# A fused scan and bilinear feed-forward kernel: pair 4's loads issued ahead of pair 0's stores, B and C of pairs 2 and 3 turned in two banks, pair 2's output copied in two halves, weights loaded in groups of three, no probe loads

## The chip, the cores and the metric

The kernel runs on one core of a Trainium2 chip. A core has four compute engines (TensorE, VectorE, ScalarE and GpSimd, in the profile PE, DVE, ACT and POOL) and SyncE (SP), which here only issues transfers. PEld is TensorE's loading of the stationary operand, which overlaps its matmuls. Each engine runs its own instructions in the order in which they were recorded, and waits on semaphores for the others. The metric is device time in microseconds, the median over runs of the whole kernel. This kernel's runs lie between 132.43 and 134.8 us.

## The reference

The first half is a gated linear recurrence (a Mamba-2 state space scan) over 4 batches of 8 heads, 768 positions, 32 channels per head and 16 states; the second is a bilinear feed-forward layer on the 3072 rows that come out.

```python
# per batch and head; log_a = log(clip(a)); chunks of positions
cum = cumsum(log_a)                       # within the chunk
M   = (C @ B.T) * exp(cum_i - cum_j) * (i >= j)
y   = M @ x + (C @ state) * exp(cum)
state = exp(sum(log_a)) * state + B.T @ (x * exp(cum_last - cum_j))
# then, with y of all heads side by side: X is 3072 x 256
out = ((X @ w_a) * (X @ w_b)) @ w_out     # w_a, w_b: 256 x 1536; w_out: 1536 x 256
```

## The kernel before

**Tiling.** The positions are cut in 6 blocks of 128. A *pair* is one block of two batches: pair p is block p // 2 of batches 2(p % 2) and 2(p % 2) + 1, so there are 12 pairs, 0 to 11, and pair p needs the state that pair p - 2 left. The decays are turned into factors (`fB`, `fC`), with which B and C are scaled; the rest is matmuls.

**What is done for one pair.** In this order, by function:

- `load(p)`: six transfers on SP's queue, two each of B (`bn`), C (`cn`) and x (`xn`), 64 KB, 64 KB and 128 KB. They go to a pool with three buffers of each.
- `scale(p)`: three GpSimd instructions, in this order: C times its factor (`cm`), B times its factor (`bm`), x to 16 bits (`x16`).
- `transposes(p)`: four TensorE transposes, B's two (`bm`) and then C's two (`cm`), into PSUM; then copies to SBUF: `BT` by two ScalarE instructions, one for each parity of the head, and `CT` by one. In the loop all three are on ScalarE. For pairs 2 and 3 `CT` is copied first, by VectorE (`ct_first`). B and C lie in the same PSUM bank, the first of the tile `SC0`.
- `scores(p)`: 32 small matmuls into the four banks of `SC0` and `SC1` (`SC[0]` to `SC[3]`; two banks belong to one tile).
- `mask(product(p, m))`: four instructions of 128x512, causal mask times scores, on VectorE. For pairs 0 to 2 one of the four goes by ScalarE (`tmp`) and GpSimd.
- `pv(p)`: scores times x, plus C times the old state (`Sbd`), into the two banks of `SC1`, and the new state's sum (`ds_mm`); then one ScalarE instruction of 128x512 copies the result to `X2T`.
- `state(p)`: two small VectorE instructions (`U32`) and two on GpSimd (`Sbd`, and `gU` for the pair after the next).
- `unit(p, k2)`, k2 from 0 to 5: four matmuls of 128x256 with `Wa` and four with `Wb` for two of the 12 tiles of hidden columns, a ScalarE copy of the first result (`asb`), and the VectorE product `hk`, which is `times`.
- `out_mm` and `out_store`: 12 matmuls of `hk` with `Wo` for each of the two batches of the pair, a ScalarE copy (`osb`) and a store on SP's queue.

**Order.** The order on each engine is written out by hand. From pair 3 on a loop interleaves the scores and masks of pair p with units of pair p - 1 and the output of pair p - 2; ahead of it, pairs 0 to 2 have their own straight-line order (lines 505 to 625), which the change touches. SP's queue there issues, in this order: pair 2's x, `load(3)`, the two stores of pair 0, `load(4)`, and then in the loop's first pass `load(5)`.

**Waits.** The layer that records the instructions adds the semaphores. For PSUM it works by tile: of two engines that use one tile the later waits for the earlier, also where both only read.

**Weights.** `Wa`, `Wb` and `Wo` come by GpSimd's queue in halves, and are turned from 32 to 16 bits on the way. The 12 tiles of 128 hidden columns are interleaved: partition c of tile k is a column of the weights so chosen that the rows of `w_out` that a partition takes lie side by side in memory. For `Wo` that is six rows (6 KB) for a partition and half; for `Wa` and `Wb` it means that the 128 weights of a partition which a matmul takes as its stationary operand lie six elements (12 bytes) apart.

**Probes.** Line 577 issues seven transfers of 64 bytes a row on SP's queue, ahead of pair 2's x. They go to a tile that nothing reads; the first waits for pair 1's x.

Of the kernel before, what the change touches and what calls it, by code (L numbers as in the profile page):

```python
# [9 lines left out]
f32 = mybir.dt.float32  # L10
f16 = mybir.dt.float16
u32 = mybir.dt.uint32
AF = mybir.ActivationFunctionType
ALU = mybir.AluOpType
PSUM = bass.MemoryType.PSUM
AFTER = mybir.DependencyInfo(mybir.DependencyClass.Sync, mybir.DependencyReason.DATA)

XS = 1024.0
YS = 16.0
# [3 lines left out]
def kernel(  # L23
# [13 lines left out]
    nc = tc.nc  # L37
# [27 lines left out]
    const = ctx.enter_context(tc.tile_pool(name="const", bufs=1))  # L65
# [16 lines left out]
    Wo = big.tile([128, NK, d_model], f16, name="Wo")  # L82
    X2T = big.tile([128, NP, 2, 2, Q], f16, name="X2T")
# [21 lines left out]
    SC1 = ps4.tile([128, 2, 512], f32, name="SC1")  # L105
    SC = [SC0[:, 0], SC0[:, 1], SC1[:, 0], SC1[:, 1]]
# [7 lines left out]
    def tiles(p):  # L114
        Bn = inp.tile([128, H, 2, N], f32, name="bn", tag="bn")
        Cn = inp.tile([128, H, 2, N], f32, name="cn", tag="cn")
        Xn = inp.tile([128, H, 2, D], f32, name="xn", tag="xn")
        pair_in[p] = (Bn, Cn, Xn)

    def load1(eng, p, which, bt, i0=0, n=64):  # L120
        blk, bp = divmod(p, NBP)
        src = (B, C, x)[which][2 * bp + bt, :, blk * Q + 2 * i0 : blk * Q + 2 * i0 + 2 * n, :]
        return eng.dma_start(
            pair_in[p][which][64 * bt + i0 : 64 * bt + i0 + n].rearrange("i h r n -> i h (r n)"),
            src.rearrange("h (i r) n -> i h (r n)", r=2),
        )

    def load(p, eng=None):
        tiles(p)
        return [load1(eng or nc.sync, p, w, bt) for w in range(3) for bt in range(2)]  # L130

    def load_w(half):
        c = slice(half * KC, (half + 1) * KC)
        return [
            nc.gpsimd.dma_start(W[half], src.rearrange("(f p) e -> p f e", p=128)[:, :, c])
            for W, src in ((Wa, moe_w_a), (Wb, moe_w_b))
        ]

    def load_wo(half):
        nc.gpsimd.dma_start(  # L140
            Wo[:, 6 * half : 6 * half + 6].rearrange("p kk e -> p (kk e)"),
            moe_w_out.rearrange("(g p kk) e -> p g (kk e)", p=128, kk=6)[:, half],
        )

    nc.sync.dma_start(a_sb, a.rearrange("b h (k q) -> (b h) k q", q=Q))
    for p_ in range(3):
# [16 lines left out]
        out=sel,  # L163
        in_=sel,
# [9 lines left out]
        out=ident, in_=ident, compare_op=ALU.is_equal, fill=0.0, base=0, pattern=[[-1, 128]], channel_multiplier=1  # L174
    )
    nc.gpsimd.memset(causal, 1.0)
    for bt in range(2):
        v = causal[64 * bt : 64 * bt + 64]
        nc.gpsimd.affine_select(  # L179
            out=v, in_=v, compare_op=ALU.is_ge, fill=0.0, base=0, pattern=[[-1, 2], [1, Q]], channel_multiplier=-2  # L180
# [1 line left out]
    load1(nc.gpsimd, 1, 0, 1)  # L182
    load1(nc.gpsimd, 1, 1, 0)
    load_w(0)
    x1 = [load1(nc.gpsimd, 1, 2, bt) for bt in range(2)]

    def warmup(n, bank, cols=512):
        for _ in range(n):
# [66 lines left out]
        scale_bc(p, 0, nc.gpsimd)  # L255
        scale_x(p, nc.gpsimd)

    def transposes(p, ps=None, between=None, ct_first=False):
        s = st[p]
        TB, TC = (TT[:, 0:256], TT[:, 256:512]) if ps is None else [t_.bitcast(f16)[:, 0:256] for t_ in ps]  # L260
        for T_, src in ((TB, s["bm"]), (TC, s["cm"])):
            for r in range(2):
                nc.tensor.transpose(  # L263
                    T_[:, r * 128 : (r + 1) * 128], src[:, r].rearrange("p h n -> p (h n)"), ident
                )
            if between:
                between()
                between = None
        BT = mid.tile([128, 2, 2, 2, 64], f16, name="bt", tag="bt")
        CT = mid.tile([128, 2, Q], f16, name="ct", tag="ct")  # L270

        def ct(copy):
            copy(CT.rearrange("p t (i r) -> p r (t i)", r=2), TC.rearrange("p (r c) -> p r c", r=2))

        if ct_first:
            ct(nc.vector.tensor_copy)
        for e in range(2):
            o_ = BT[:, e].rearrange("p r t i -> p (r t i)")
            nc.scalar.activation(out=o_, in_=TB, func=AF.Copy, scale=par[:, e : e + 1])  # L279
        if not ct_first:  # L280
            ct(nc.scalar.copy if ps is None else nc.vector.tensor_copy)
        s["BT"], s["CT"] = BT, CT

    def scores(p):
# [18 lines left out]
    def product(p, m):  # L303

        return (
            st[p]["T1"][:, 2 * m : 2 * m + 2].rearrange("p e r q -> p e (r q)"),
            SC[m].rearrange("p (e c) -> p e c", e=2),
        )
# [8 lines left out]
    def mask(out_in, by_pool=False):  # L317
        o_, i_ = out_in
        c_ = causal.rearrange("p r q -> p (r q)").unsqueeze(1).broadcast_to((128, 2, 2 * Q))
        if by_pool:  # L320
            tmp = mid.tile([128, 2, 2 * Q], f32, name="tmp", tag="tmp")
            nc.scalar.copy(tmp, i_)  # L322
            nc.gpsimd.tensor_tensor(out=o_, in0=tmp, in1=c_, op=ALU.mult)  # L323
        else:
            nc.vector.tensor_tensor(out=o_, in0=i_, in1=c_, op=ALU.mult)  # L325
# [32 lines left out]
                        tile_position=(64 * bt, 32 * m),  # L358
                    )

    def pv(p, then=None):
        blk, bp = divmod(p, NBP)
        s = st[p]
        PY = [SC1[:, bt, 0:256] for bt in range(2)]
        if blk > 0:
            for bt in range(2):
                for u in range(2):
                    nc.tensor.matmul(  # L368
                        PY[bt][:, u * Q : (u + 1) * Q],
                        s["Sbd"][:, bt, u * 128 : u * 128 + 128],  # L370
                        s["CT"][:, bt],
                        start=(u == 0),
                        stop=False,
                        skip_group_check=True,
                    )
        for u in range(2):
            pv_u(p, u, PY, blk == 0)
        if blk < NBLK - 1:
            ds_mm(p, 256)
        if then:  # L380
            then()
        nc.scalar.activation(  # L382
            out=X2T[:, p].rearrange("p u t q -> p t u q"),
            in_=SC1[:, :, 0:256].rearrange("p t (u q) -> p t u q", u=2),
            func=AF.Copy,
            scale=YS / XS,
        )

    def evac0(u, bt, eng, py):
        o_, i_ = X2T[:, 0, u, bt], py[bt][:, u * Q : (u + 1) * Q]  # L390
# [40 lines left out]
    def unit_mm(p, k2, W):  # L431
        ps = psf.tile([128, 512], f32, name="aps" if W is Wa else "bps", tag="ff")
        for kk in range(2):
            k = 2 * k2 + kk
            for f in range(2):
                nc.tensor.matmul(  # L436
                    ps[:, kk * 2 * Q : (kk + 1) * 2 * Q],
                    W[k // 6][:, f].rearrange("p (c kk) -> p kk c", kk=6)[:, k % 6],
                    X2T[:, p, f].rearrange("p t q -> p (t q)"),
                    start=(f == 0),  # L440
                    stop=(f == 1),
                    skip_group_check=True,
                )
        return ps

    def evac_a(a_ps, on_dve=False):
        asb = ffh.tile([128, 512], f32, name="asb", tag="asb")
        (nc.vector.tensor_copy if on_dve else nc.scalar.copy)(asb, a_ps)  # L448
        return asb

    def times(p, k2, b_ps, asb):
        s = st[p]
        if "hk" not in s:
            s["hk"] = ffh.tile([128, NK, 2 * Q], f16, name="hk", tag="hk")
        nc.vector.tensor_tensor(  # L455
            out=s["hk"][:, 2 * k2 : 2 * k2 + 2, :].rearrange("p k q -> p (k q)"), in0=b_ps, in1=asb, op=ALU.mult
        )

    def unit(p, k2):
        a_ps = unit_mm(p, k2, Wa)  # L460
        b_ps = unit_mm(p, k2, Wb)
        asb = evac_a(a_ps)
        return lambda: times(p, k2, b_ps, asb)
# [35 lines left out]
    def go(*items):  # L499
        for p, k2 in items:  # L500
            unit(p, k2)()

    def pull(p):
        if ("S", p) in st:
            st[p].update(st.pop(("S", p)))
# [56 lines left out]
    for bt in range(2):  # L562
# [6 lines left out]
        out=hsx,  # L569
        in0=hs.unsqueeze(1).broadcast_to((BH, nb, NG)),  # L570
        in1=selb.rearrange("p (b g) -> p b g", b=nb),
        op=ALU.mult,
    )
    load_wo(1)
    pz = const.tile([16, 7, 16], f32, name="pz")
    for i, k in enumerate((14, 12, 10, 8, 6, 4, 2)):
        d = nc.sync.dma_start(pz[0:k, i], moe_w_a[0:k, 0:16])
        if i == 0:
            tc.add_manual_dep(d.ins, x1[1].ins.name, AFTER, reason="probe")
    x2 = [load1(nc.sync, 2, 2, bt) for bt in range(2)]  # L580
    tc.add_manual_dep(x2[0].ins, w1[1].ins.name, AFTER, reason="weights ahead of pair 2's x")
    for m in range(3):
# [19 lines left out]
    state_spread(1)  # L602
    load(3)
    go((0, 3), (0, 4), (1, 3), (0, 5))
    transposes(2, ct_first=True)
    go((1, 4), (1, 5))
    scores(2)
    mask(product(2, 3), by_pool=True)
    for m in range(3):
        mask(product(2, m))  # L610
    scale_x(2, nc.scalar)
    scale(3)
    o = [bank("ops"), bank("ops")]
# [1 line left out]
        for bt in range(2):  # L615
            out_mm(0, bt, o[bt], ks)
    pull(2)
    pv(2)
    for bt in range(2):
        out_store(0, bt, o[bt])  # L620
    transposes(3, ct_first=True)
    state(2)
    fb(2)
    load(4)
    go((2, 0))

    for p in range(3, NP):
# [5 lines left out]
        h = unit(p - 1, 0) if p > 3 else None  # L633
# [5 lines left out]
        h = unit(p - 1, 1)  # L639
# [56 lines left out]
```

## Time and profile before

| | |
|---|---|
| median of 13 runs | 133.66 us (132.43 to 134.8) |
| the profiled execution, its own time | 133.81 us |
| its span (first to last instruction) | 132.1 us |
| TensorE busy with matmuls | 121.6 us, 92% of the span |
| VectorE, ScalarE, GpSimd busy | 88.2, 74.1, 57.5 us |
| granted TensorE clock | 1.0 of full speed |

The profile is of one execution. A row of the timeline gives the start in us from the span's start, the duration, the engine, the line of the kernel, the operation, the tiles (out, then in), the shape and count, and in brackets for how long the engine stood idle before it and what ended that. A row of the waits gives who waited for what: us in total, times, longest. The chain of waits goes back from the last instruction: at each step to what released it, or else to the instruction before it on its engine. A row of the windows gives each engine's busy time in a stretch.

### The profile page before, as it was taken

To read this page: it belongs to the slowest core of one execution; us is meant where nothing else is said; L and a number is where in the kernel's file an instruction comes from. 1 tells how busy PE (TensorE), PEld (TensorE's weight loads), DVE (VectorE), ACT (ScalarE), POOL (GpSimd) and SP (SyncE) were. 2 spreads that over 40 slices of the span, in tenths; PEclk is the share of its full clock that TensorE was granted. 3 is DMA by queue.
4 is the path that set the end of the run, shared out by engine and by line. 5 is a ranking of instruction groups with operands and counts; after the bars stand their busy time and mean duration, and the time that the engine had idled before them with its cause. 6 is when DMAs were issued, how large, how long until landed. Compare 5 with 4: busy or idle time off the path is not lost.

```text
span 132.1 us, 4745 instructions
## 1 busy us (share of the span) xinstructions
PE 121.6 (92%) x1951; PEld 108.2 (82%) x1951; DVE 88.2 (67%) x166; ACT 74.1 (56%) x152; POOL 57.5 (44%) x81
## 2 busy tenths in 40 slices
PE   6886899997959999999999999999999999999980
PEld 2444699886949999998999999999999899899970
DVE  2786877684970984974975956957939929744440
ACT  1554666556446648557566476576575485465420
POOL 6999586657338706608409319119047000000000
PEclk9999999999999999999999999999999999999999
DMA  3999999961466563541542443614511010110102
GB/s 72 182 129 220 174 179 113 202 129 34 98 130 113 144 126 94 88 113 45 92 111 65 79 105 72 124 49 88 113 45 45 28 51 5 40 40 5 51 29 79
DMA packets 39189, 12.22 MB, mean 93 GB/s; under 512 B 34592, under 2 KB 38720, under 8 KB 39168
## 3 DMA queue, kind: packets, MB, share of 16 engines
q1 hardware_dynamic: 34944, 8.42, 28.7%
q0 software_dynamic: 1696, 3.02, 13.9%
q10 hardware_dynamic: 2528, 0.49, 1.9%
q8 instruction: 15, 0.25, 0.8%
q14 instruction: 6, 0.05, 0.1%
HBM read 11.14 MB, written 3.15 MB: 108 GB/s over the span
## 4 chain that ended last, share of the span: by engine, by line
PE 77%; DMA 7%; DVE 5%; POOL 4%; issue 2%; ACT 2%; SPq 0%; POOLq 0%; ACTq 0%
PE aps L436 24%; PE bps L436 21%; PE ops L468 21%; DMA Wa<-in_moe_w_a_dram 5%; DVE t L325 3%; PE SC L292 3%; PE SC L334 3%; PE SC L263 2%; DMA cn<-in_C_dram 2%; PE SC L368 2%; PE SC L351 1%; DVE hk L455 1%; ACT bt L279 1%; POOL causal L179 1%; PE fps L215 1%
## 5 line engine op out<-in xcount | busy, mean ns | idle before, releaser
L455 DVE TENSOR_TENSOR hk<-bps,asb 128x512 f16<-128x512 f32 x72 | 49.1, 688 | 27.8 <-ACT asb L448 25.0
L448 ACT COPY asb<-aps 128x512 f32<-128x512 f32 x71 | 41.6, 587 | 20.0 <-PE aps L436 11.8
L436 PE MATMUL aps<-X2T,Wa 128*128 128x256 f16 x288 | 43.4, 274 | 1.5 <-DMA Wa<-in_moe_w_a_dram 1.1
L436 PE MATMUL bps<-X2T,Wb 128*128 128x256 f16 x288 | 42.9, 273 | 0.0
L468 PE MATMUL ops<-Wo,hk 128*128 128x256 f16 x288 | 35.0, 273 | 0.0
L436 PEld LDWEIGHTS <-Wa 128*128 128x128 f16 x288 | 31.7, 126 | 3.0 <-DMA Wa<-in_moe_w_a_dram 1.4
L436 PEld LDWEIGHTS <-Wb 128*128 128x128 f16 x288 | 32.5, 125 | 0.2 <-DMA Wb<-in_moe_w_b_dram 0.2
L468 PEld LDWEIGHTS <-hk 128*128 128x128 f16 x288 | 27.7, 98 | 3.1
L325 DVE TENSOR_TENSOR t<-SC,causal 128x512 f16<-128x512 f32 x45 | 29.3, 681 | 1.0 <-PE SC L292 1.0
L416 POOL TENSOR_TENSOR sbd<-U,maskbd 128x512 f16<-128x512 f32 x10 | 11.6, 1165 | 30.5 <-DVE U L409 24.9
L483 ACT ACTIVATE osb<-ops 128x256 f32<-128x256 f32 x23 | 8.7, 385 | 15.8 <-PE ops L468 15.7
L239 POOL TENSOR_SCALAR x<-xn 128x512 f16<-128x512 f32 x9 | 13.4, 1492 | 1.8 <-DMA xn<-in_x_dram 1.3
L382 ACT ACTIVATE X2T<-SC 128x512 f16<-128x512 f32 x11 | 6.6, 597 | 9.1 <-PE SC L351 8.1
L279 ACT ACTIVATE bt<-SC,ch 128x256 f16<-128x256 f16 x22 | 9.2, 474 | 2.9 <-PE SC L263 1.8
L245 POOL TENSOR_TENSOR cm<-cn,fC 128x256 f16<-128x256 f32 x10 | 6.2, 623 | 5.8 <-DMA cn<-in_C_dram 5.8
L245 POOL TENSOR_TENSOR bm<-bn,fB 128x256 f16<-128x256 f32 x11 | 7.0, 640 | 0.4 <-DMA bn<-in_B_dram 0.4
L409 DVE SCALAR_TENSOR_TENSOR U<-SC,G,gU 128x64 f32<-128x64 f32 x16 | 3.9, 280 | 4.2 <-ACT X2T L382 4.1
L292 PE MATMUL SC<-ct,bt 32*64 32x128 f16 x384 | 5.1, 220 | 0.8 <-ACT bt L279 0.5
L292 PEld LDWEIGHTS <-bt 32*64 32x64 f16 x384 | 3.5, 104 | 2.9 <-issue 2.4
L334 PEld LDWEIGHTS <-x 64*32 64x32 f16 x384 | 3.3, 91 | 2.9 <-issue 0.6
L189 PE MATMUL SC<-warm 128*128 128x512 f16 (+1 forms) x15 | 4.4, 435 | 1.2 <-DVE warm L159 1.2
L323 POOL TENSOR_TENSOR t<-tmp,causal 128x512 f16<-128x512 f32 x3 | 3.5, 1158 | 4.4 <-ACT tmp L322 4.3
(65 smaller groups left out, 76.0 us busy)
## 6 DMA issues: line engine op xcount, KB each, us to landing
out_dram<-osb SPq DMA_DIRECT2D x23, 128.0 KB, 1.8
xn<-in_x_dram SPq DMA_DIRECT2D x21, 128.0 KB, 7.1
bn<-in_B_dram SPq DMA_DIRECT2D x20, 64.0 KB, 2.4
cn<-in_C_dram SPq DMA_DIRECT2D x18, 64.0 KB
Wa<-in_moe_w_a_dram POOLq DMA_DIRECT2D x2, 384.0 KB, 6.9
Wb<-in_moe_w_b_dram POOLq DMA_DIRECT2D x2, 384.0 KB, 8.1
Wo<-in_moe_w_out_dram POOLq DMA_DIRECT2D x2, 384.0 KB, 7.0
xn<-in_x_dram POOLq DMA_DIRECT2D x2, 128.0 KB, 7.2
```

The source lines that it names most:

```text
L239: eng.tensor_scalar(xo, xi, XS, None, ALU.mult)
L245: eng.tensor_tensor(out=m_, in0=pair_in[p][which].rearrange("p h r n -> p r h n"), in1=f[:, blk, :, bp].unsqueeze(3).broadcast_to((128, 2, ...
L279: nc.scalar.activation(out=o_, in_=TB, func=AF.Copy, scale=par[:, e : e + 1])
L292: nc.tensor.matmul(SC[m][64 * bt : 64 * bt + 64, c0 : c0 + Q], BT[rows, e, r, bt], CT[rows, bt], start=True, stop=True, skip_group_check=True,
L325: nc.vector.tensor_tensor(out=o_, in0=i_, in1=c_, op=ALU.mult)
L334: nc.tensor.matmul(py[bt][32 * g : 32 * g + 32, u * Q : (u + 1) * Q], s["X16"][k, h, r, :], s["T1"][k, h, r, :], start=(first and u == 0 a ...
L416: nc.gpsimd.tensor_tensor(out=Sbd.rearrange("p t (m c) -> p t m c", m=4), in0=U32[:, p].unsqueeze(2).broadcast_to((128, 2, 4, 2 * D)), in1 ...
L436: nc.tensor.matmul(ps[:, kk * 2 * Q : (kk + 1) * 2 * Q], W[k // 6][:, f].rearrange("p (c kk) -> p kk c", kk=6)[:, k % 6], X2T[:, p, f].rea ...
L448: (nc.vector.tensor_copy if on_dve else nc.scalar.copy)(asb, a_ps)
L455: nc.vector.tensor_tensor(out=s["hk"][:, 2 * k2 : 2 * k2 + 2, :].rearrange("p k q -> p (k q)"), in0=b_ps, in1=asb, op=ALU.mult)
L468: nc.tensor.matmul(o_ps[:, 0:d_model], hk[:, k, bt * Q : (bt + 1) * Q], Wo[:, k, :], start=(k == 0), stop=(k == NK - 1), skip_group_check= ...
L483: nc.scalar.activation(out=o_sb, in_=o_ps[:, 0:d_model], func=AF.Copy, scale=1.0 / (YS * YS))
```

## The change

- `load(4)` is recorded before the two stores of pair 0, and so stands before them in SP's queue.
- `transposes` takes `apart` in place of `ct_first`. For pairs 2 and 3, with `apart=True`, B is turned into `SC[0]` and C into `SC[1]`, which are the two banks of the tile `SC0`; `BT` is copied by ScalarE, and after it is recorded the copy of `CT` on VectorE.
- `pv(2)` copies its result in two instructions of 128x256, the first by ScalarE and the second by VectorE.
- `transposes(3)` is recorded before pair 0's `osb` copies, which puts the `BT` copies before them on ScalarE.
- Unit (1, 5)'s VectorE product (`h()`) comes after the first of pair 2's VectorE masks, in place of before all three.
- The weights' interleaving goes by three rather than six: the stationary operands' elements lie three elements (6 bytes) apart, and a half of `Wo` is 128 times two pieces of 3 KB rather than 128 of 6 KB.
- The seven probe loads are gone.

```diff
     def load_wo(half):
         nc.gpsimd.dma_start(
-            Wo[:, 6 * half : 6 * half + 6].rearrange("p kk e -> p (kk e)"),
-            moe_w_out.rearrange("(g p kk) e -> p g (kk e)", p=128, kk=6)[:, half],
+            Wo[:, 6 * half : 6 * half + 6].rearrange("p (g kk) e -> p g (kk e)", kk=3),
+            moe_w_out.rearrange("(g p kk) e -> p g (kk e)", p=128, kk=3)[:, 2 * half : 2 * half + 2],
         )
...
-    x1 = [load1(nc.gpsimd, 1, 2, bt) for bt in range(2)]
+    for bt in range(2):
+        load1(nc.gpsimd, 1, 2, bt)
...
-    def transposes(p, ps=None, between=None, ct_first=False):
+    def transposes(p, ps=None, between=None, apart=False):
         s = st[p]
+        if ps is None:
+            ps = [SC[0], SC[1]] if apart else None
+            on_dve = apart
+        else:
+            on_dve = True
         TB, TC = (TT[:, 0:256], TT[:, 256:512]) if ps is None else [t_.bitcast(f16)[:, 0:256] for t_ in ps]
...
-        def ct(copy):
-            copy(CT.rearrange("p t (i r) -> p r (t i)", r=2), TC.rearrange("p (r c) -> p r c", r=2))
-
-        if ct_first:
-            ct(nc.vector.tensor_copy)
         for e in range(2):
             o_ = BT[:, e].rearrange("p r t i -> p (r t i)")
             nc.scalar.activation(out=o_, in_=TB, func=AF.Copy, scale=par[:, e : e + 1])
-        if not ct_first:
-            ct(nc.scalar.copy if ps is None else nc.vector.tensor_copy)
+        (nc.vector.tensor_copy if on_dve else nc.scalar.copy)(
+            CT.rearrange("p t (i r) -> p r (t i)", r=2), TC.rearrange("p (r c) -> p r c", r=2)
+        )
...
-    def pv(p, then=None):
+    def pv(p, then=None, split=False):
...
-        nc.scalar.activation(
-            out=X2T[:, p].rearrange("p u t q -> p t u q"),
-            in_=SC1[:, :, 0:256].rearrange("p t (u q) -> p t u q", u=2),
-            func=AF.Copy,
-            scale=YS / XS,
-        )
+        o_ = X2T[:, p].rearrange("p u t q -> p t u q")
+        i_ = SC1[:, :, 0:256].rearrange("p t (u q) -> p t u q", u=2)
+        if split:
+            nc.scalar.activation(out=o_[:, 0], in_=i_[:, 0], func=AF.Copy, scale=YS / XS)
+            nc.vector.tensor_scalar(o_[:, 1], i_[:, 1], YS / XS, None, ALU.mult)
+        else:
+            nc.scalar.activation(out=o_, in_=i_, func=AF.Copy, scale=YS / XS)
...
-                    W[k // 6][:, f].rearrange("p (c kk) -> p kk c", kk=6)[:, k % 6],
+                    W[k // 6][:, f, k % 6 // 3 * 384 : (k % 6 // 3 + 1) * 384].rearrange("p (c kk) -> p kk c", kk=3)[
+                        :, k % 3
+                    ],
...
-    pz = const.tile([16, 7, 16], f32, name="pz")
-    for i, k in enumerate((14, 12, 10, 8, 6, 4, 2)):
-        d = nc.sync.dma_start(pz[0:k, i], moe_w_a[0:k, 0:16])
-        if i == 0:
-            tc.add_manual_dep(d.ins, x1[1].ins.name, AFTER, reason="probe")
...
-    transposes(2, ct_first=True)
-    go((1, 4), (1, 5))
+    transposes(2, apart=True)
+    go((1, 4))
+    h = unit(1, 5)
     scores(2)
     mask(product(2, 3), by_pool=True)
-    for m in range(3):
-        mask(product(2, m))
+    mask(product(2, 0))
+    h()
+    mask(product(2, 1))
+    mask(product(2, 2))
     scale_x(2, nc.scalar)
     scale(3)
...
-    pv(2)
+    pv(2, split=True)
+    transposes(3, apart=True)
+    load(4)
     for bt in range(2):
         out_store(0, bt, o[bt])
-    transposes(3, ct_first=True)
     state(2)
     fb(2)
-    load(4)
     go((2, 0))
```

## The prediction

> **What bounds the kernel now.** I read the page's busy rows first, then the busy tenths, then the chain of waits and the timeline where TensorE is not full.
>
> ```profile
> span 132.1 us, 4745 instructions
> PE 121.6 (92%) x1951; PEld 108.2 (82%) x1951; DVE 88.2 (67%) x166; ACT 74.1 (56%) x152; POOL 57.5 (44%) x81
> PE   6886899997959999999999999999999999999980
> ...
> L436 PE MATMUL aps<-X2T,Wa 128*128 128x256 f16 x288 | 43.4, 274 | 1.5 <-DMA Wa<-in_moe_w_a_dram 1.1
> L468 PE MATMUL ops<-Wo,hk 128*128 128x256 f16 x288 | 35.0, 273 | 0.0
> L436 PEld LDWEIGHTS <-Wa 128*128 128x128 f16 x288 | 31.7, 126 | 3.0 <-DMA Wa<-in_moe_w_a_dram 1.4
> L468 PEld LDWEIGHTS <-hk 128*128 128x128 f16 x288 | 27.7, 98 | 3.1
> ```
>
> TensorE is the bound. From the 13th of the 40 slices on (about 40 us) it is full to the tail, in the order written. Nothing there waits, so a microsecond that TensorE gains before is carried whole to the end, and work that other engines lose or gain later costs nothing while it stays inside the loop's slack. What can be saved is TensorE's idle time ahead of that. The timeline and the page's waits give it between 24 and 42 us:
>
> ```profile
> 26.40 0.43 PE L292 MATMUL SC<-ct,bt 32*64 32x128 f16 x32 [0.22 <-ACT bt L279]
> 29.99 0.38 PE L368 MATMUL SC<-ct,sbd 128*128 128x128 f16 x4 [0.34 <-DVE t L325]
> 31.61 0.60 PE L436 MATMUL aps<-X2T,Wa 128*128 128x256 f16 x4 [0.40 <-ACT X2T L382]
> 32.89 0.43 PE L292 MATMUL SC<-ct,bt 32*64 32x128 f16 x32 [0.24 <-ACT bt L279]
> 38.49 0.62 POOL L245 TENSOR_TENSOR cm<-cn,fC 128x256 f16<-128x256 f32 x1 [4.48 <-DMA cn<-in_C_dram]
> 39.75 0.29 PE L263 MATMUL SC<-ident,bm 128*128 128x128 f16 x2 [1.64 <-POOL bm L245]
> ```
>
> Five stops: 0.22 + 0.34 + 0.40 + 0.24 + 1.64 = 2.84 us. The largest is pair 4's transposes, which wait for GpSimd's `bm`, and GpSimd stood 4.48 us for C of pair 4. Why that came late shows in SP's own rows:
>
> ```profile
> 26.74 1.27 SPq L123 DMA_DIRECT2D xn<-in_x_dram  x2
> 31.86 0.86 SPq L485 DMA_DIRECT2D out_dram<-osb  x2
> 32.82 1.48 SPq L123 DMA_DIRECT2D bn<-in_B_dram  x2
> 34.40 1.85 SPq L123 DMA_DIRECT2D cn<-in_C_dram  x2
> ...
> 30.00:31.00 1.00, 1.00 (x56) 0.85 (x56) 0.00 (x0) 0.04 (x1) 0.28 (x2) 1.00 0.03 7
> 31.00:32.00 1.00, 0.60 (x8) 0.51 (x6) 0.75 (x3) 1.00 (x4) 1.00 (x1) 1.00 0.00 0
> ```
>
> SP has issued pair 3's x by 28.0 and then stands until 31.86 for pair 0's `osb`, with `load(4)` behind it. In the windows of 30 to 31 and 31 to 32 us the DMA share (the last figure but one) is 0.03 and 0.00: the transfers are idle just then.
>
> **Load(4) ahead of the stores.** Its six issues move past two stores on SP; no other queue changes order. They then start at about 28.1. The semaphores in the built program ask for nothing late: buffers of pair 1 (free since 15.6), and that pair 2's x and pair 3's B and C have landed (used without a wait at 27.66, 29.57 and 28.99). With the 1.3 to 1.5 us per pair of issues of the rows above, C's second issue starts at about 30.2; before, it started at about 35.6 and landed 2.73 later (chain of waits). So C lands at about 33, or 34 if it queues behind pair 3's x, which landed at 30.9. GpSimd is busy until 34.02 anyway (`sbd`, `gU`). Then `cm` and `bm`, 0.62 each: `bm` is ready at 35.3. TensorE wants it at about 37.6. The 1.64 us go, with 2.3 us to spare. The stores now stand behind six issues that end at 32.5, and their data comes at 32.1: no cost, since nothing waits for a store until its `osb` buffer is reused two passes later. `load(5)` follows at 33.4 rather than 37.8. What is late next is pair 4's scores, after 1.31 + 1.75 us of other matmuls; ScalarE needs 0.60 + 0.84 + 0.46 for `X2T`, `BT`, `CT`, so no wait follows.
>
> **Two banks, two engines.** Here the semaphores matter more than the banks.
>
> ```profile
> 25.03 0.44 DVE L273 COPY ct<-SC 128x256 f16<-128x256 f16 x1
> 25.51 0.84 ACT L279 ACTIVATE bt<-SC,ch 128x256 f16<-128x256 f16 x2 [1.12 <-DVE ct L273]
> ```
>
> Before, ScalarE stood 1.12 us for VectorE's read of the same bank. The Trainium skill (PSUM — Partial Sum Buffer, "PSUM bank collisions raise a hardware error") says that two engines must not use one bank and the same partitions together, even to read, while different banks are free. By that page BT and CT from two banks would run together. But in the built program the `CT` copies of pairs 2 and 3 still wait for ScalarE's second `BT` copy, since both banks are one tile: BT comes first, CT after it, and only the order is turned. VectorE's half of `X2T` touches the same two banks as ScalarE's half, so there page and program agree: it waits for it. With the page's freedom for BT and CT, pair 3's scores would come 0.1 us earlier; I count by the program.
>
> *Pair 2.* BT starts at 24.48 (after the transposes and the `asb` copy that ends at 24.39), ends 25.32; CT 25.36 to 25.80. The 0.22 stop goes and scores start at 26.18. ScalarE is free of BT earlier, so `asb` (1,4) ends at 25.80 and (1,5) at 26.34, against 26.8 and 27.3. VectorE: product (1,4) at 25.85, mask 0 from 26.67, product (1,5), masks 1 and 2, at 0.60 a step and 0.68 for the last: to 29.15. TensorE, 0.22 ahead, is through with the output matmuls at 29.43 (29.65 before). So `pv(2)` starts at 29.43, not 29.99: 0.56 us gained.
>
> *X2T of pair 2.* pv takes 0.89, to 30.32. Before, ScalarE's one copy took 0.60. Now two in series: ScalarE's half by the nearest row, `osb` of 128x256, 0.385; a semaphore of 0.05 (31.56 to 31.61 above); VectorE's half by its `osb` row, 0.425. Starting 0.08 after pv, it ends at 31.27, and units of pair 2 start at 31.32 against 31.61: 0.27 of the 0.56 is given back. If the halves did run together it would be 30.9.
>
> *Pair 3.* `BT` now precedes `osb` on ScalarE: 30.72 to 31.56. `CT` to 32.05, `U32` twice to 32.43 (0.47), and the scores write that tile, so they start at about 32.45, against 32.89: 0.44 gained. The `osb` copies end at 32.1, `asb` at 32.57, product at 32.65; from there to pair 3's last mask 3.68 as before (33.34 to 37.02), so 36.33, ahead of pv(3) at 37.22 - 0.44 = 36.78. Pair 3's own transposes are near: `bm` was ready at 30.19, and they would now start at 30.25. If C of pair 3 delays it, up to 0.4 of this is lost. Bounds of this part: 0 to 0.8; I take 0.44.
>
> **Weights by three.** The rows: 126 ns for a load at a stride of 12 bytes, 98 for `hk`, which is contiguous. The skill (SBUF — State Buffer, "Door 1: The DMA port swizzle", the note on cachelines) says that reads need at least two hits per 16-byte line: 12 bytes give 1.3, 6 bytes 2.7. Applied to all 576 loads that would be 576 x 28 ns = 16 us. The trace speaks against counting it so: matmuls of both kinds follow each other at 0.109 us (0.44 for 4 and 1.31 for 12 in the chain), so a load of 126 is hidden as well as one of 98. Only the first load after the small matmuls of the scores is bare (0.57 for 4 instead of 0.44), about once a pair: 10 x 28 ns = 0.28 at most. Bounds 0 to 0.28, and a loss if the odd stride reads worse (below); I take 0.1. `Wo` in 3 KB pieces has the shape of `Wa`'s and `Wb`'s, which take 6.9 and 8.1 us to landing against 7.0: between 0 and 1.1 us later. Its second half was issued at 18.9, landed at about 26, and is first read at about 28: covered by 2 us. Beyond that it stalls.
>
> **Probes.** SP issues them at 14.62 to 17.04 and then waits to 19.41 for `Wb` in any case, so x of pair 2 starts no sooner. Worth 0; without that cover it would be the 2.4 us of their issues on SP, of which TensorE would see little, since x of pair 2 waited for ScalarE, not ScalarE for it.
>
> **The sum.** 1.64 + 0.44 + 0.1 = 2.18 us. The profiled execution (span 132.1, with 1.7 around it, 133.81) lies 0.15 above the median; 133.66 - 2.18 = 131.5 us.
>
> **Rivals.**
> 1. *Only the load pays.* The series of halves costs 0.3 more than counted, or pair 3's C holds its transposes: the front gives 0, the end 133.66 - 1.64 = 132.0. For it: the waits in the built program. Against: scores of pair 3 waited for BT, which now starts a full 1.2 us earlier.
> 2. *The wait comes back.* Pair 4's loads share the engines with pair 3's x and land no earlier than 37, or the next wait (pair 5's, pair 4's scores) takes the place: then some 0.5 of the 1.64 stays, and with a poor front the end is 133.1 or above, no change. Against: DMA share 0.0 at 30 to 32.
> 3. *Slower: the odd stride.* If 6 bytes (every second weight off a 4-byte boundary) reads slower, not faster, than 12, a load may no longer hide behind a matmul. It decides from a spacing of 109 + 2180/576 = 113 ns: each nanosecond beyond costs 0.58 us; 120 would give 135.5. Against: 98 contiguous and 126 at 12 bytes, with nothing in the trace between.
> 4. *Each engine reads its bank in parallel after all*, against the waits: 131.0.
>
> **How the numbers follow.** A run of this kernel tells about 0.5% (0.67 us) from no change. The forecast has 0.60, rival 4 0.06, rival 1 0.18, rival 2 0.09, rival 3 0.05, a late `Wo` 0.02. Faster: forecast, rivals 4 and 1: 0.84. No change, mostly rival 2: 0.09. Slower 0.07. The range runs from 130.6 (front 0.8, all bare loads gained, 0.3 for the spread of a median) to 132.6 (rival 1 with a part of rival 2).
>
> **What would show it.** Right: the timeline after has `bn` of pair 4 issued on SP at 28 to 29, before the first `out_dram`; `cm` at about 34 with no DMA wait; pair 4's transposes without an idle bracket at about 37.6. `ct` of pairs 2 and 3 still begins after `bt` ends, and the VectorE half of `X2T` after ScalarE's; the stop before pair 2's first `aps` grows from 0.40 to about 0.67 while its start moves to 31.3. Loads of `Wa` drop below 126 ns with matmuls still at 0.109. Wrong: an idle bracket above 0.5 at pair 4's transposes or scores, matmuls spaced above 0.112, or an `ops` matmul waiting for `Wo`.

## The result and the profile after

The changed kernel's median is 131.69 us (130.36 to 134.66, 11 runs) against 133.72 for the kernel before (48 runs): a ratio of 0.9855, with a 95% interval of 0.9825 to 0.9886, or 1.9 us (1.5 to 2.3). The forecast was 131.5. The ratio leaves out two runs of the changed kernel in which the granted clock was low (134.66 us at 0.987, 132.35 at 0.973) and such runs of the kernel before; the medians count them. In a second comparison, run with the last experiments below, the same kernel had 0.9883 (0.9847 to 0.9919).

The profiled execution has a span of 129.8 us against 132.1. From its page: span, busy time, tenths of TensorE, and the groups of the loads and matmuls.

```profile
span 129.8 us, 4737 instructions
PE 121.5 (94%) x1951; PEld 104.3 (80%) x1951; DVE 88.5 (68%) x167; ACT 74.0 (57%) x152; POOL 57.9 (45%) x81
PE   6989499998999999999999999999999999999980
...
L438 PE MATMUL aps<-X2T,Wa 128*128 128x256 f16 x288 | 43.1, 273 | 0.7 <-DVE X2T L387 0.6
L472 PE MATMUL ops<-Wo,hk 128*128 128x256 f16 x288 | 35.1, 273 | 0.0
L438 PEld LDWEIGHTS <-Wa 128*128 128x128 f16 x288 | 28.7, 103 | 3.7 <-issue 0.8
L472 PEld LDWEIGHTS <-hk 128*128 128x128 f16 x288 | 27.7, 98 | 3.2
```

TensorE does nearly the same work (121.5 us, 121.6 before) in 2.3 us less; of the two thin slices between 29 and 40 us (7 and 5) an 8 is left. The new thin one (4, at 13 to 16 us) comes from a late transfer, of which more below. The timeline of the changed kernel has these rows for the points at which TensorE stood before (pair 2's scores, pv of pair 2, the first unit of pair 2, pair 3's scores, GpSimd's C of pair 4, pair 4's transposes):

```profile
26.50 0.43 PE L293 MATMUL SC<-ct,bt 32*64 32x128 f16 x32
29.54 0.38 PE L369 MATMUL SC<-ct,sbd 128*128 128x128 f16 x4
31.40 0.60 PE L438 MATMUL aps<-X2T,Wa 128*128 128x256 f16 x4 [0.65 <-DVE X2T L387]
32.36 0.58 PE L293 MATMUL SC<-ct,bt 32*64 32x128 f16 x32
34.63 0.62 POOL L246 TENSOR_TENSOR cm<-cn,fC 128x256 f16<-128x256 f32 x1
37.65 0.29 PE L269 MATMUL SC<-ident,bm 128*128 128x128 f16 x2
```

Only the first unit of pair 2 still has a bracket, and it has grown from 0.40 to 0.65. SP's rows say why pair 4's C no longer holds GpSimd: its loads are issued from 27.30 on, before the stores.

```profile
27.30 1.27 SPq L123 DMA_DIRECT2D bn<-in_B_dram  x2
28.69 2.09 SPq L123 DMA_DIRECT2D cn<-in_C_dram  x2
30.95 1.27 SPq L123 DMA_DIRECT2D xn<-in_x_dram  x2
32.32 1.05 SPq L489 DMA_DIRECT2D out_dram<-osb  x2
```

The difference of 2.3 us is the sum of four figures of the two timelines: when pair 2's transposes start, and three stretches behind that, each from the start of one TensorE row to the next: from pair 2's transposes to pv(3), from there to pair 4's transposes, from there to the end of the span.

| | start, pair 2's transposes | to pv(3) | to pair 4's transposes | to the end |
|---|---|---|---|---|
| before | 24.04 | 13.18 | 2.53 | 92.35 |
| changed | 24.43 | 12.39 | 0.83 | 92.15 |
| difference | +0.39 | -0.79 | -1.70 | -0.20 |

The first column does not come from the edits to the order. ScalarE's scaling of pair 1's x shows what is behind it; the first row is of the kernel before, the second of the changed one.

```profile
14.98 0.64 ACT L237 ACTIVATE x<-xn 128x512 f16<-128x512 f32 x1
15.72 0.63 ACT L238 ACTIVATE x<-xn 128x512 f16<-128x512 f32 x1 [1.44 <-DMA xn<-in_x_dram]
```

That transfer landed later in this execution. Three kernels below are the same program as the changed one up to there (X2T in one copy, one copy with CT first, load(4) between the stores), and in their profiles ScalarE waited for it 0.21 us or not at all. Over all profiles of this study, before and after the change, pair 2's transposes start anywhere from 22.83 to 25.55 us. The stretches are therefore better compared than the spans.

### The profile page after: what moved, and what is told of

It reads as the page before. It is cut to its first block, busy times and chain, and to the rows that moved or that the text cites. A ratio compares the mean times of both kernels' runs of the same rounds, so it can differ in the third digit from the quotient of the medians.

```text
span 129.8 us, 4737 instructions
## 1 busy us (share of the span) xinstructions
PE 121.5 (94%) x1951; PEld 104.3 (80%) x1951; DVE 88.5 (68%) x167; ACT 74.0 (57%) x152; POOL 57.9 (45%) x81
## 4 chain that ended last, share of the span: by engine, by line
PE 84%; DMA 6%; POOL 5%; ACT 1%; DVE 1%; issue 1%; ACTq 0%; POOLq 0%
PE ops L472 24%; PE aps L438 24%; PE bps L438 23%; DMA xn<-in_x_dram 6%; PE SC L335 3%; PE SC L293 3%; PE SC L269 2%; PE SC L369 2%; PE SC L352 1%; POOL causal L179 1%; PE fps L216 1%; POOL ch L171 1%; POOL Wb L135 1%; POOL Wa L135 1%; POOL bn L123 1%
## 5 line engine op out<-in xcount | busy, mean ns | idle before, releaser
L438 PEld LDWEIGHTS <-Wa 128*128 128x128 f16 x288 | 28.7, 103 | 3.7 <-issue 0.8
L438 PEld LDWEIGHTS <-Wb 128*128 128x128 f16 x288 | 29.6, 103 | 2.1 <-DMA Wb<-in_moe_w_b_dram 0.4
L389 ACT ACTIVATE X2T<-SC 128x512 f16<-128x512 f32 x10 | 6.0, 597 | 6.2 <-PE SC L352 5.2
L335 PE MATMUL SC<-t,x 64*32 64x128 f16 x352 | 4.6, 219 | 1.6 <-ACT x L238 1.6
```

What stands on the lines that cost most here:

```text
L335: nc.tensor.matmul(py[bt][32 * g : 32 * g + 32, u * Q : (u + 1) * Q], s["X16"][k, h, r, :], s["T1"][k, h, r, :], start=(first and u == 0 a ...
L438: nc.tensor.matmul(ps[:, kk * 2 * Q : (kk + 1) * 2 * Q], W[k // 6][:, f, k % 6 // 3 * 384 : (k % 6 // 3 + 1) * 384].rearrange("p (c kk) -> ...
```

## The experiments

Ratios are to the kernel before, run on the same chip in the same rounds; the interval is 0.3 to 0.6% either way. The table reads every profile as above; "start" is that of pair 2's transposes.

| kernel | ratio (95% interval) | start | to pv(3) | to pair 4's transposes | to the end |
|---|---|---|---|---|---|
| load(4) alone | 0.989 (0.9842 to 0.9938) | 22.91 | 13.31 | 0.82 | 92.36 |
| front alone | 1.000 (0.9958 to 1.0043) | 22.83 | 13.05 | 3.11 | (94.0) |
| load(4) between the stores | 1.0005 (0.9973 to 1.0038) | 23.77 | 13.08 | 2.58 | 92.17 |
| weights by six | 0.9853 (0.9805 to 0.99) | 23.75 | 12.94 | 0.82 | 92.29 |
| X2T in one copy | 0.9861 (0.9833 to 0.9888) | 23.31 | 13.07 | 0.83 | 92.19 |
| one copy, CT first | 0.9858 (0.9812 to 0.9905) | 23.89 | 12.96 | 0.82 | 92.13 |
| probes back | 0.9904 (0.9868 to 0.994) | 25.55 | 12.43 | 0.82 | 92.2 |
| four tiles | 0.9812 (0.9764 to 0.9861) | 23.33 | 12.38 | 0.87 | 92.12 |
| four tiles, pair 3's B and C first | 0.9835 (0.9808 to 0.9863) | 24.32 | 12.07 | 0.83 | 92.18 |
| changed, beside the next two | 0.9883 (0.9847 to 0.9919) | 24.26 | 12.39 | 0.83 | 92.12 |
| four tiles again | 0.984 (0.9801 to 0.9878) | 23.32 | 12.35 | 0.88 | 92.15 |
| pair 3's B and C first again | 0.9896 (0.9833 to 0.9959) | 23.18 | 13.19 | 0.83 | 92.1 |

The last stretch of *front alone* is in brackets because its profiled execution had a granted clock of 0.985: the page's clock row shows half speed in the slice from 40 to 43 us, behind the rows that are read below. In the profile of *probes back* (0.984) the clock was low ahead of the start.

**load(4) alone.** The kernel before, with one call moved.

```diff
     pv(2)
+    load(4)
     for bt in range(2):
         out_store(0, bt, o[bt])
...
     fb(2)
-    load(4)
     go((2, 0))
```

> The kernel before with one edit: load(4) recorded ahead of pair 0's two stores. My theory (the 1.64 us stop before pair 4's transposes goes, nothing takes its place): 1.6 us faster than before, ratio about 0.988, and no idle bracket at pair 4's transposes. Rival (the load only moves the wait on, and the gain of the change is its reordered front and its weights): less than 0.7 us, with a new idle bracket on TensorE between 38 and 45 us.

Measured: 0.989, 1.5 us (0.8 to 2.1), and 0.82 us from pv(3) to pair 4's transposes, the bare length of the matmuls between. By this figure the single edit brings most of the change's gain, though the interval overlaps the changed kernel's, so the times do not tell the two apart. No new stop took the place of the one removed.

**Front alone.** The changed kernel with `load(4)` behind the stores, the weights by six and the probes, so that only the front's edits are left.

```diff
-    load(4)
     for bt in range(2):
         out_store(0, bt, o[bt])
     state(2)
     fb(2)
+    load(4)
     go((2, 0))
```

> The kernel before with the front's edits alone: B and C of pairs 2 and 3 turned in two banks and BT copied first, pair 2's output in two halves, unit (1, 5)'s product between the masks, pair 3's transposes ahead of the osb copies. load(4), the weights' grouping by six and the probes stay as before. My prediction: 0.44 us up to pv(3), from the two traces rather 0.8, but pair 4's transposes still wait for bm, whose time is set by pair 0's stores on SP; these come no earlier, since pair 0's osb copies now stand behind BT on ScalarE. So TensorE runs into the same wait earlier and stands longer there: 0 us gained at the end, perhaps 0.2 lost (ratio 1.000 to 1.002), with a bracket of about 2.3 us or more at pair 4's transposes. Rival (front and load add up independently): ratio 0.994 to 0.997.

Measured: 1.000. By itself this does not exclude the rival, whose 0.997 lies in the interval; the next kernel, with the same front, is narrower. The timeline shows where the front's gain went:

```profile
30.97 0.86 SPq L486 DMA_DIRECT2D out_dram<-osb  x2
37.74 0.62 POOL L245 TENSOR_TENSOR cm<-cn,fC 128x256 f16<-128x256 f32 x1 [4.63 <-DMA cn<-in_C_dram]
38.99 0.29 PE L268 MATMUL SC<-ident,bm 128*128 128x128 f16 x2 [2.22 <-POOL bm L245]
```

TensorE stands 2.22 us at pair 4's transposes instead of 1.64. This execution started early (22.83 against 24.04), so its times are counted from the start: pv(3) comes only 0.13 us sooner than before; the first store, whose `osb` copies now stand behind `BT` on ScalarE, is issued 0.32 us later (8.14 after the start, 7.82 before), load(4) follows behind it, and pair 4's transposes come 0.45 us later. So the front's gain and the load's do not add up one by one: without the load the front showed no gain.

**load(4) between the stores.** Everything of the change but this: SP still waits for one `osb`.

```diff
-    load(4)
-    for bt in range(2):
-        out_store(0, bt, o[bt])
+    out_store(0, 0, o[0])
+    load(4)
+    out_store(0, 1, o[1])
```

> The changed kernel with load(4) between pair 0's two stores in place of ahead of both, so that SP still waits for the first osb before it issues load(4), at about 32.5 us in place of 27.3. My theory (that one wait is the whole of the 1.64 us, and the load needs some 6 us from its issue to bm): the stop before pair 4's transposes comes back with 1 to 2 us, and 1 to 2 us are lost against the changed kernel. Rival (it is the transfer of the stores, or the place in the queue, that delays the load): less than 0.5 us lost.

Measured: 1.0005; all of the gain is gone. As this kernel has the front's edits too, its interval leaves them at most 0.36 us while the load is late. The timeline of this kernel, SP, GpSimd and TensorE:

```profile
31.96 0.37 SPq L489 DMA_DIRECT2D out_dram<-osb  x1
32.44 1.27 SPq L123 DMA_DIRECT2D bn<-in_B_dram  x2
38.18 0.62 POOL L246 TENSOR_TENSOR cm<-cn,fC 128x256 f16<-128x256 f32 x1 [4.08 <-DMA cn<-in_C_dram]
39.43 0.28 PE L269 MATMUL SC<-ident,bm 128*128 128x128 f16 x2 [1.69 <-POOL bm L246]
```

SP was through with pair 3's x at 28.3 and stood to 31.96. The stores' transfers are not what costs (one of them now lies behind the load): the wait for the first `osb`, at the head of an in-order queue, is.

**Weights by six.** The changed kernel with `kk=6` in `load_wo` and in the matmul's operand, as before.

```diff
-                    W[k // 6][:, f, k % 6 // 3 * 384 : (k % 6 // 3 + 1) * 384].rearrange("p (c kk) -> p kk c", kk=3)[
-                        :, k % 3
-                    ],
+                    W[k // 6][:, f].rearrange("p (c kk) -> p kk c", kk=6)[:, k % 6],
```

> The changed kernel with the weights grouped by six again, for Wa, Wb and Wo. My theory (all but about ten weight loads are hidden behind matmuls): 0.1 to 0.3 us slower than the changed kernel, loads of Wa and Wb back at 125 ns, matmuls still 0.109 us apart, the first four after the scores 0.57 instead of 0.55. Rival (the line rule applied to every load, or Wo's smaller pieces cost): several us slower, or faster by some tenths.

Measured: 0.9853, not told apart from the changed kernel by time. The rows tell it apart. First the groups of the kernel with six; then a piece of the chain of waits with six, and the same piece with three (the changed kernel): start, length, what.

```profile
L438 PE MATMUL aps<-X2T,Wa 128*128 128x256 f16 x288 | 43.3, 274 | 0.2 <-DVE X2T L387 0.2
L438 PEld LDWEIGHTS <-Wa 128*128 128x128 f16 x288 | 31.8, 126 | 1.5 <-issue 0.3
```

```profile
50.73 0.57 PE aps L438 x4
51.31 0.44 PE bps L438 x4
```

```profile
50.85 0.55 PE aps L438 x4
51.40 0.44 PE bps L438 x4
```

A load takes 126 ns with six and 103 with three, 98 when contiguous. Behind a matmul none of it shows (0.44 for four either way). Bare, after the scores, it is 0.02 us, once a pair. The last stretch agrees: 92.35, 92.36 and 92.29 with six (front alone left out), 92.10 to 92.20 in all with three, 0.1 to 0.2 us apart where the spans are given to 0.1. That is under what the runs' times can tell.

**X2T in one copy.** `pv(2)` in place of `pv(2, split=True)`.

```diff
-    pv(2, split=True)
+    pv(2)
```

> The changed kernel with pair 2's X2T copied by ScalarE in one instruction, as before. The halves in series cost 0.24 us at pair 2's first unit (0.65 of idle against 0.40). My theory: the idle there falls back to about 0.4, but BT, CT and U32 of pair 3 then start later, since CT waits for BT and BT for the whole X2T, so pair 3's scores wait instead: pv(3) within 0.2 us of the changed kernel's, no difference that can be measured. Rival (the split is a plain loss of 0.24 to 0.27): 0.25 us faster than the changed kernel.

Measured: 0.9861, beside the changed kernel's 0.9855. The rival's 0.25 us is 0.2%, less than the intervals, so the time does not exclude it. In the profile the idle before the first unit is gone because pair 3's transposes now hold TensorE ahead of it (0.58, for `bm`); the scores of pair 3 then stand for CT:

```profile
29.91 0.29 PE L269 MATMUL SC<-ident,bm 128*128 128x128 f16 x2 [0.58 <-POOL bm L246]
31.72 0.78 PE L293 MATMUL SC<-ct,bt 32*64 32x128 f16 x32 [0.54 <-DVE ct L280]
```

**One copy, CT first.** In addition pair 3's CT is copied by VectorE while ScalarE copies X2T.

```diff
-    pv(2, split=True)
-    transposes(3, apart=True)
+    pv(2)
+    transposes(3, apart=True, ct_first=True)
```

> The changed kernel with pair 2's X2T in one ScalarE instruction and pair 3's CT copied by VectorE ahead of BT, while X2T is being copied. My theory (what holds pair 3's scores is the chain X2T, BT, CT, U32 in series): 0.6 us from pv's end to the first aps and no stop at the scores, pv(3) 0.2 us earlier relative to pv(2) than in the changed kernel, 0.2 us at the end where pair 3's bm does not hold the transposes. Rival: bm of pair 3 comes last in any case, so that nothing changes.

Measured: 0.9858, no difference, though 0.2 us could not have been seen. The profiled execution stood 0.42 at `bm` and then 0.34 at BT. It speaks for the rival: with a start as early as here (23.89) `bm` of pair 3 holds the transposes, and the order of the copies behind it moved pv(3) by little (12.96, beside 12.94 with weights by six, which stood about as long at `bm`).

**Probes back.** Line 577's seven loads on SP again.

```diff
+    pz = const.tile([16, 7, 16], f32, name="pz")
+    for i, k in enumerate((14, 12, 10, 8, 6, 4, 2)):
+        d = nc.sync.dma_start(pz[0:k, i], moe_w_a[0:k, 0:16])
```

> The changed kernel with the seven probe loads put back. My theory: 0.0 us, since SP waits for Wb behind them in any case; x of pair 2 is issued at the landing of Wb in both. Rival (they hold back the transfers behind them): 0.2 us or more slower, pair 3's C landing later than in the changed kernel.

Measured: 0.9904, with an interval that overlaps the changed kernel's (0.9825 to 0.9886). Pair 2's x is issued at 19.43 here and between 18.56 and 19.86 in the profiles of the changed kernel and its variants without the probes, so SP's queue is not held back. This profile's stretches are the changed kernel's; only its start is late (25.55). The clock row of its page gives part of the cause:

```profile
PEclk9999977999999999999999999999999999999999
```

At 16 to 23 us the granted clock was 0.74, and four matmuls of a unit took 0.85 us instead of 0.44; before that, pair 1's x had kept ScalarE waiting for 1.12 us. This execution (132.71 us) is one of the six in the ratio. Three other kernels with the probes (before, load(4) alone, front alone) started at 22.83 to 24.04, so the late start is not shown to be the probes' doing. Zero and a cost of half a per cent both remain possible.

**Four tiles.** Each PSUM bank as a tile of its own. The edit also takes pair 0's masks by bank (the diff leaves that out) and, in the other pairs, copies X2T in two instructions.

```diff
-    SC0 = ps4.tile([128, 2, 512], f32, name="SC0")
-    SC1 = ps4.tile([128, 2, 512], f32, name="SC1")
-    SC = [SC0[:, 0], SC0[:, 1], SC1[:, 0], SC1[:, 1]]
+    SC = [ps4.tile([128, 512], f32, name=f"SC{i}") for i in range(4)]
...
+        i_ = [PY[t].rearrange("p (u q) -> p u q", u=2) for t in range(2)]
+        nc.scalar.activation(out=o_[:, 0], in_=i_[0], func=AF.Copy, scale=YS / XS)
         if split:
-            nc.vector.tensor_scalar(o_[:, 1], i_[:, 1], YS / XS, None, ALU.mult)
+            nc.vector.tensor_scalar(o_[:, 1], i_[1], YS / XS, None, ALU.mult)
         else:
-            nc.scalar.activation(out=o_, in_=i_, func=AF.Copy, scale=YS / XS)
+            nc.scalar.activation(out=o_[:, 1], in_=i_[1], func=AF.Copy, scale=YS / XS)
```

> The changed kernel with the four PSUM banks as four tiles of their own, so that the built program lets ScalarE and VectorE read different banks at the same time: BT and CT of pairs 2 and 3 together, and pair 2's X2T in two halves by bank. In the other pairs ScalarE copies X2T in two instructions of 128x256, and pair 0's masks go by bank. My theory (the tile made them wait in series): pair 2's units start 0.4 us after pv's end instead of 0.9, pair 3's scores 0.4 us earlier, and about 0.3 us is left at the end, since VectorE's masks of pair 3 then hold pv(3): 131.4 us against 131.7. Rival (the hardware lets the two engines' reads slow each other, or the series was hidden): no change at the end, the halves in parallel take longer than 0.385 and 0.43 us each.

Measured: 0.9812. First the rows of the changed kernel, in which the two engines take turns; then those of four tiles.

```profile
30.50 0.38 ACT L386 ACTIVATE X2T<-SC 128x256 f16<-128x256 f32 x1 [2.33 <-PE SC L352]
30.79 0.84 ACT L279 ACTIVATE bt<-SC,ch 128x256 f16<-128x256 f16 x2
30.92 0.43 DVE L387 TENSOR_SCALAR X2T<-SC 128x256 f16<-128x256 f32 x1 [1.44 <-ACT X2T L386]
31.66 0.45 DVE L280 COPY ct<-SC 128x256 f16<-128x256 f16 x1 [0.32 <-ACT bt L279]
```

```profile
29.37 0.38 ACT L383 ACTIVATE X2T<-SC 128x256 f16<-128x256 f32 x1 [2.21 <-PE SC L350]
29.48 0.42 DVE L385 TENSOR_SCALAR X2T<-SC 128x256 f16<-128x256 f32 x1 [1.12 <-PE SC L350]
29.92 0.29 PE L267 MATMUL SC<-ident,bm 128*128 128x128 f16 x2 [0.62 <-POOL bm L244]
30.24 0.84 ACT L277 ACTIVATE bt<-SC,ch 128x256 f16<-128x256 f16 x2 [0.49 <-PE SC L267]
30.35 0.45 DVE L278 COPY ct<-SC 128x256 f16<-128x256 f16 x1 [0.45 <-PE SC L267]
```

From two banks the engines read side by side at the same lengths (0.38 and 0.42; 0.84 and 0.45): it was the tile that put them in series, not the hardware. The gain stands at pair 3's scores. They start 1.21 us after pair 3's transposes here (29.92 to 31.13), and 1.81 after them with weights by six and with X2T in one copy, which stood for `bm` as well; to pv(3) it is 12.38 against 12.94 and 13.07. The idle before pair 2's first unit is gone too, but the stop at `bm` ahead of it is enough for that: load(4) between the stores has two banks to a tile, stood 0.62 there, and shows none either. For the same reason the 0.4 us from pv's end to that unit, which were expected, are not seen here (0.85).

**Pair 3's B and C ahead of pair 2's x**, with four tiles.

```diff
+    tiles(3)
+    bc3 = [load1(nc.sync, 3, w, bt) for w in range(2) for bt in range(2)]
+    tc.add_manual_dep(bc3[0].ins, w1[1].ins.name, AFTER, reason="weights ahead of pair 3's B")
     x2 = [load1(nc.sync, 2, 2, bt) for bt in range(2)]
-    tc.add_manual_dep(x2[0].ins, w1[1].ins.name, AFTER, reason="weights ahead of pair 2's x")
...
-    load(3)
+    for bt in range(2):
+        load1(nc.sync, 3, 2, bt)
```

> The kernel with four PSUM tiles, and pair 3's B and C issued on SP ahead of pair 2's x rather than behind it. In the runs whose start was early (transposes of pair 2 at 22.8 to 23.8 us) pair 3's transposes stood 0.45 to 0.62 us for bm, which waited for C of pair 3. My theory (that landing is the next stop): this idle goes, GpSimd's cm of pair 3 has no DMA wait, and the end is 0.3 to 0.6 us earlier than with the four tiles alone. Rival (x of pair 2 then lands too late for pv(2), or the transfers are bound by their total): the idle moves to pv(2) or stays, no gain or a loss of up to 1 us.

Measured: 0.9835, beside 0.9812 of the four tiles alone. This profile has no idle at `bm`, but it started late (24.32), and with such a start the changed kernel has none either. The stretch to pv(3) is the shortest of all (12.07); no profile of the four tiles alone started as late, so how much of that is the order's is not shown.

**Side by side.** The last three were run on one chip, to compare them with each other.

> The changed kernel once more, on the chip of the two kernels with four PSUM tiles, for a comparison side by side: ratio to before about 0.985.

> The kernel with four PSUM tiles once more, beside the changed kernel: 0.3 to 1.0 us faster than it, if the gain seen before was no accident of an early start; no difference otherwise.

> Four PSUM tiles and pair 3's B and C ahead of pair 2's x once more, beside both: 0.2 to 0.5 us faster than the four tiles alone if the landing of pair 3's C is the next stop in most runs; equal if the late landing of pair 1's x sets the time in as many.

Measured: 0.9883, 0.984 and 0.9896. Four tiles came out 0.4% below the changed kernel in both comparisons, about half a microsecond (medians 130.52 and 130.86 against 131.69 and 131.42; weights by six, run beside the first, had 131.45). The intervals overlap, so it is the likely best, not a certain one. Pair 3's loads first shows no gain over it. In its second profile, with an early start (23.18), `bm` no longer holds TensorE, but another stop stands just ahead:

```profile
29.84 0.42 PE L333 MATMUL SC<-t,x 64*32 64x128 f16 x32 [1.20 <-ACT x L236]
```

Pair 2's x, now issued behind pair 3's B and C, lands too late for pv(2). With an early start, either order of these transfers holds TensorE.

## Why the prediction was right

- *TensorE is full from 40 us on, so what is gained before is kept.* Shown: 92.35 us before and 92.15 after, from pair 4's transposes to the end.
- *Load(4) takes away the 1.64 us.* Shown by the one edit (0.82 us left in the stretch) and by its undoing (1.69 of idle back, ratio 1.0005). The dates held: issue forecast at 28.1, found at 27.30; `bm` forecast ready at 35.3, found at 35.82 (35.20 + 0.62); transposes at 37.6, found at 37.65. Rival 2 did not come about.
- *The banks bring nothing, the tile decides.* Shown: CT began after BT, VectorE's half of X2T after ScalarE's, the idle before the first unit grew to 0.65 (forecast about 0.67). The rule that the prediction took from the Trainium skill (PSUM — Partial Sum Buffer, "PSUM bank collisions raise a hardware error"), different banks are free, describes the hardware; the four tiles show it at work. Rival 4 was wrong for this kernel. What the freedom of BT and CT would bring at pair 3's scores, 0.1 by the forecast, was 0.15 with a late start (1.85 after the transposes with four tiles and pair 3's B and C first, 2.00 in the changed kernel) and 0.6 where `bm` held the transposes.
- *The front, 0.44.* This is the term that was mis-sized. With a late start, as in the changed kernel's two profiles (24.43 and 24.26), it is 0.79: pair 2's scores came 0.29 sooner after the transposes and not 0.22, the output matmuls followed the scores after 0.36 and not 0.48, which the sum did not have, and pv(2) followed them 0.43 sooner and not 0.34. With a start before 24 us it is 0.1 to 0.24 against the kernel before (13.18 to 13.08 and 12.94), or 0.23 to 0.37 against load(4) alone (13.31), which has the old front and also started early; `bm` of pair 3 then holds the transposes. The prediction named this as what could cost it up to 0.4 us, and as part of rival 1, but gave that only 0.18; five of the eight profiles that have its front and two banks to a tile show a stop of 0.42 to 0.62 there (not the changed kernel's own two, nor the one with the probes, which started at 24.26 or later). The loss and the surplus stand on both sides of 0.44, so that the sum came out near is in part luck; which start is the usual one, the few profiles do not tell. Nor do the runs' times exclude the rest of rival 1: load(4) alone has 0.989, with an interval that overlaps the changed kernel's. That the front and the weights add something to it is read from the stretches.
- *The parts as a sum.* The prediction added front and load as if each stood alone. Front alone gave 1.000, and with the load between the stores 1.0005: its gain counts only where the load is early as well. For the whole change, where the load is early, adding was right.
- *Weights, 0.1.* 0.1 to 0.2 by the last stretch, within the bounds of 0 to 0.28. The 16 us that the line rule cited in the prediction (SBUF — State Buffer, "Door 1: The DMA port swizzle") would make of all loads are excluded, and so is rival 3: 103 ns, faster than 126. One sum of rival 3 is wrong, without effect on the forecast: at a spacing of 120 ns the loss is 11 ns a matmul, 6.3 us over 576, which makes 137.8 and not 135.5. `Wo` in smaller pieces was landed before it was read: the matmuls that take it stood for nothing (0.0 in their group).
- *Probes, 0.* Not settled to better than half a per cent.

## What to carry to other kernels

A load behind a store in an in-order queue waits for the store's data; look in the queue's rows for a stretch in which it issues nothing while the transfers are idle. Before counting on two engines reading in parallel, read in the built program what each waits for: a layer that tracks whole tiles puts them in series where the banks would be free. And where two waits are met one after the other, and what ends the second does not come sooner with the first, a gain at the first is nothing until the second is gone.

## What the runs showed of the hardware

- The start varies more than most of the effects here: pair 2's transposes began between 22.83 and 24.43 us across the profiles at a full clock until then, and at 25.55 in the one whose clock had been 0.74 at 16 to 23 us. What pair 3 needs does not come sooner by as much: in the seven profiles in which GpSimd waited for its C (starts of 22.83 to 23.89) it went on 5.16 to 5.36 us after the start, at 28.14 to 29.13; in the changed kernel's two and the one with the probes, which started at 24.26 to 25.55, it took C without a wait 4.40 to 4.58 us after the start. So an early start is partly lost at pair 3.
- A 128x128 weight load took 126 ns with elements 12 bytes apart, 103 at 6 bytes and 98 contiguous, and all three were hidden where matmuls of 128x256 follow each other: these came 0.109 us apart with each.
- ScalarE and VectorE read two PSUM banks at once without slowing each other (0.38 and 0.42 us side by side, 0.38 and 0.43 in series).
